# Six borrowed exponential tiles, shared first casts and marks, a later first v, and a new order of engines and transfers in a fused routing-attention and gated feed-forward kernel

## The chip, the core and the metric

The kernel runs on one core of a Trainium2 chip. A core has a matrix engine (TensorE, "PE" in the profile; "PEld" is its weight load), a vector engine (VectorE, "DVE"), a scalar engine (ScalarE, "ACT"), a general engine (GpSimd, "POOL") and an engine that issues most transfers (SyncE, "SP"). Each engine works through its own list of instructions in order; semaphores tie the lists together. The metric is the device time of one execution in microseconds (us). Where several executions are compared, the median counts.

## The reference

Attention with 4 batches, 8 heads, 768 tokens and 64 columns per head. A query sees only those keys whose nearest centroid (of 16 per head) is its own. The result, 3072 rows of 512 columns, goes through a feed-forward layer with a softmax gate and a layer norm.

```python
q_assign = np.argmax(np.einsum('bhsd,hcd->bhsc', q_n, c_n), axis=-1)
k_assign = np.argmax(np.einsum('bhsd,hcd->bhsc', k_n, c_n), axis=-1)
mask = q_assign[:, :, :, None] == k_assign[:, :, None, :]
scores = np.where(mask, scale * np.matmul(q, k.transpose(0, 1, 3, 2)), -1000000000.0)
attn = softmax(scores);  x = matmul(attn, v) as rows of 512
h = x @ w_in                                  # 512 -> 1024
solu = h * softmax(h)
ln = (solu - mu) / np.sqrt(var + 1e-06) * g_ln
return ln @ w_out                             # 1024 -> 512
```

## The kernel before

**Routing inside the matmul.** The kernel builds no mask. Under the 64 columns of q and k it puts 16 rows that hold a 1 at the token's own cluster, so that one matmul with 80 (or 96) contraction rows gives the score plus a large bias where the clusters agree. These rows are called marks here.

**The steps and their names.** Two heads form a pair, so there are 16 pairs, numbered batch.pair. The text `ORDER` names each step by two or three letters, and gives for each engine the order in which its steps are issued; `Weave.queues` (L111) turns a text into a list, and `Weave.run` (L125) emits the steps by a planned start. The table `AWAY` (L74) moves single steps to another engine than their usual one. What stands in `ORDER` is therefore the order on the chip.

| step | what it does | lines |
|---|---|---|
| `ld`, `lv`, `lo`, `li`, `lg` | loads of q and k, v, w_out, w_in, g_ln | L367-403, L526, L548-566 |
| `tp`, `xa` | batch 0: transposes of q or k on PE into the region `hreg`, and the copy to `xt` | L383, L390 |
| `xt` | later batches: transpose on DVE | L405 |
| `ca` | cast of `xt` into the score operand `qk` | L424 |
| `cp`, `cb`, `cq`, `cf` | transposes of the centroids and the two copies made of them | L863-878 |
| `cl`, `tb`, `mx`, `oh`, `ot`, `pl`, `bl` | assignment: scores against centroids, transpose, maximum, one-hot, transpose back, the marks put in place (`place`, L499), a blank | L439-524 |
| `S`, `E`, `V`, `N` | score bank, exponential, attention times v, normalisation | L595-650 |
| `tx`, `h`, `hm`, `ex`, `u`, `tu`, `bn`, `ag`, `at`, `al`, `y`, `sc`, `ou` | the feed-forward part of one block of 128 rows | L678-802 |
| `su`, `sk`, `me`, `ce`, `wi` | w_out centred, w_in cast | L552-590 |
| `fl`, `wm` | idle matmuls | L818, L858 |

**How it is tiled.** There are 294 score banks `S` with as many exponentials `E`, 192 products `V`, and 24 feed-forward blocks. The first 24 banks (pair 0.0) have 384 columns, the other 270 have 512. A score bank is a PSUM tile of a ring of three, so `S` number i waits for `E` number i-3 (L1037). An exponential goes to a tile of a ring of nine in SBUF (`ep`, L212), so `E` number i waits for the `V` that read number i-9 (L1042). `cl`, `cp`, `cq` and `y` share a single PSUM bank (`ps_m`), which a `y` holds until its `sc`.

**The start.** Pair 0.0 is treated in two halves of 384 tokens, so that its first score banks can begin early. The prologue (L805-857) issues the eight small loads of q and k on SP and ACT and then `load_v(0, 0)` (L811). For each half, two transposes and two copies lead to `cl`, then to `tb`, `mx`, `oh` and `ot` on DVE, and then to four marks `pl` (two of k, two of q). In the kernel before, every bank of the first half needs all four (L1033):

```python
            nd |= {f"pl{ts[1 - x]}.{x}.{part}" for x in range(2)
                   for part in ((hh,) if apart(b, p) else range(2))}
```

**Order.** For all engines the order is written out by hand in `ORDER` (L28-73). Each queue is in order: a step that waits holds all steps behind it on its engine.

Of the kernel before, what the change touches and what calls it, by code (L numbers as in the profile page):

```python
# [11 lines left out]
BF16 = mybir.dt.bfloat16  # L12
# [10 lines left out]
class Weave:  # L23
# [6 lines left out]
        ld4 lv si ld4 lv lg ld4 lv2 ld4 lo2 ld4 lo ld3 lo ld3 li4 tx ld3 lv3 tx ld4 tu ld9 lv ld tu  # L30
        tx ld3 tu ld3 ou ld2 ou ld tu ld12 tu ld4 lv ld2 ou tx ld3 tu ou ld2 tx lv ld tu ld4 tx ld
        tu ou2 ld lv ld4 tu ld4 tu ld ou ld7 pl ou ld lv2 ld3 tu lv tx ou tu lv pl ld4 ou2 tx lv tu
        tx ou tu pl2 tu2 tx tu tx ou2 tx ou tu tx2 ou tu2 ou2 tu2 ou6
    """
    ORDER["POOL"] = """
        po z ca2 pl2 cv z bl pl2 ca z ca pl2 ca z2 ca3 cv ca cv ca pl3 sg ca cv2 pl3 ca2 gs pl ca cv
        ca wi ca pl2 wi3 bl ca pl2 cv at cv pl ca pl al bl at cv ca pl ca pl cv ca3 al at ca al ca
        at ca pl2 bl cv pl2 ca4 at ca2 al ca pl2 bl pl2 cv2 ca3 al at pl2 bl pl2 ca pl al ca3 at cv
        at pl ca pl2 ca2 pl al cv2 bl cv2 pl2 ca pl al pl at al at pl2 ca3 at al bl cv pl2 bl cv2
        ca3 pl5 al cv3 at al ca2 cv ca cv ca2 at ca2 pl ca al pl2 at2 pl3 at ca cv al at2 al2 at2 al  # L40
        at al3 at al2 at2 al2
    """
    ORDER["PE"] = """
        wm tp2 cp tp cl tp fl5 cl fl4 S3 tp2 S2 tp S cq S tp S2 tp2 S2 V3 S cl S tp2 V3 S gt S tp S
        tp S2 cl S2 V2 S V S2 tp S2 tp S2 V2 S V S2 cl S2 V2 S V2 S3 V S2 V2 S2 V S cl S3 su S2 V3 S
        V S3 V3 S2 V S su S2 V S V3 S3 me S3 V4 S3 cl S3 V4 S2 h S h S2 h S h S2 V3 S2 V h S h V S V
        S h S V S V S h S2 V3 S2 V h S2 h V2 S y3 S2 h3 S3 y V3 h V S2 V2 S cl S3 h2 S2 V3 S y2 S V
        h2 S V y2 S h S V h S2 h S y3 S2 y V3 h S3 cl V2 S V S y S2 y2 S3 V3 S y S2 V3 S2 cl S V S2
        V2 S h S2 V2 S V S h S2 V2 cl V2 S3 y2 S V S2 V y S2 y V2 S3 h2 S V h S h S2 V h S V S V y2
        S h V y2 S2 V S h3 S cl V S2 V2 S h V cl S3 h2 V y V S3 y2 V S h V3 S y S h S2 h2 S3 V2 y h  # L50
        S V S2 y V3 y S3 h3 y S3 V3 S h S V S V cl S V S h S cl V2 S3 y V2 S y S2 y V2 S3 h y V S3 V
        h V2 S3 cl S2 V2 S y3 S2 y S V3 S V S y S2 V S V3 S2 y2 S3 y V2 S2 h V2 S3 h3 S V S2 V y S V
        h2 V2 S y S2 y V y S h2 S3 cl h V S2 V3 S h V2 S3 h2 S y S2 V h S2 V y2 V4 S3 y h S2 h V h V
# [12 lines left out]
        u ag N cv hm sc bn u N hm ag bn N bn u bn2 hm ag2 N bn u bn2 N ag hm bn u N ag hm bn2 u bn2
        hm sc u N ag2 bn tx hm bn sc u bn ag hm bn tu ag u2 bn2 ag sc
    """
    ORDER["ACT"] = """
        wa xa2 ca2 xa ca2 E12 xa2 E6 xa E58 ex E12 ex E8 ex E8 ex E3 sc E5 ca E2 ex E25 ex E9 sc E6  # L70
        ex E5 sc E2 ex E9 ex E8 ex E9 sc E6 ex E18 ex E21 ex E5 sc E3 ex E9 ex E7 sc E2 ex E7 ex E8
        ex E7 ex E6 sc E ex E2 sc E3 ex E2 sc ex sc ex sc ex tu sc tu2 sc2 oz
# [3 lines left out]
        ca0.0.0.0.0 ca0.0.0.1.1 ca1.3.1.1 sc23.0 tu22.1 tu23.1 xa0.0.1.0 xa0.2.1.0 xa0.2.1.1  # L76
        xa0.3.0.0
    """.split(), "ACT"))
    AWAY.update(dict.fromkeys("""
        bl0.0.1 bl2.2 bl3.1 bl3.2 bl3.3 ca0.0.1.0.0 ca0.1.1.0 ca1.0.0.1 ca3.1.1.0 cv0.0.0 cv0.2.0  # L80
        cv1.2.0 cv2.0.0 cv3.3.0 pl0.0.0.1.1 pl0.1.0.0 pl0.2.1.1 pl0.3.0.0 pl0.3.0.1 pl0.3.1.0 sc0
        sc10 sc13 sc17 sc19 sc2 sc23.1 sc3 sc6 sc8 sc9 tu22.0 zo
    """.split(), "DVE"))
    AWAY.update(dict.fromkeys("""
        ca0.0.1.1.1 pl0.0.0.1.0 pl0.0.1.0.0 pl0.0.1.1.0 pl1.0.0.0 pl1.0.0.1 pl1.0.1.0 pl1.0.1.1
        pl1.1.0.0 pl1.1.0.1 pl1.1.1.0 pl1.1.1.1 pl1.2.0.0 pl1.2.0.1 pl1.2.1.0 pl1.2.1.1 pl1.3.0.0
        pl1.3.0.1 pl1.3.1.0 pl1.3.1.1 pl2.0.0.0 pl2.0.0.1 pl2.0.1.0 pl2.0.1.1 pl2.1.0.0 pl2.1.0.1
        pl2.1.1.0 pl2.1.1.1 pl2.2.0.0 pl2.2.0.1 pl2.2.1.0 pl2.2.1.1 pl2.3.0.0 pl2.3.1.0 pl2.3.1.1
        pl3.0.0.0 pl3.0.0.1 pl3.0.1.0 pl3.0.1.1 pl3.1.0.1 pl3.1.1.0 pl3.1.1.1 pl3.2.0.0 pl3.2.0.1
        pl3.2.1.0 pl3.3.0.1 pl3.3.1.0 pl3.3.1.1  # L90
# [79 lines left out]
def kernel(  # L170
# [328 lines left out]
    def place(b, p, hf, i, part, e):  # L499
# [6 lines left out]
        if apart(b, p):  # L506
            ins = VEC[e].tensor_copy(
                side(b, p, i, part, slice(0, S))[D:D + NC_].bitcast(F32)
                .rearrange("p (t u n) -> p u t n", t=n_t // 2, u=2),
                asg[b, p, hf, "oht"][r.start:r.start + NC_].bitcast(F32)  # L510
                .rearrange("p (u t n) -> p u t n", t=n_t // 2, u=2))
        elif e == "SP":
            ins = nc.sync.dma_start(out=dst, in_=src.unsqueeze(1).to_broadcast([NB, 2, n]))
        else:
            ins = VEC[e].tensor_copy(dst.bitcast(F32), src.bitcast(F32).unsqueeze(1)  # L515
                                     .to_broadcast([NB, 2, n // 2]))
# [76 lines left out]
    es, sps_, opss, xs = {}, {}, {}, {}  # L593

# [10 lines left out]
    def expo(n, k):  # L605
        w = wide(n, k)
        es[n, k] = ep.tile([P, 512], BF16, name="e")
# [203 lines left out]
    load_v(0, 0)  # L811
# [47 lines left out]
    for j in range(sum(int(x or 1) for x in re.findall(r"\bfl(\d*)", wv.ORDER.get("PE", "")))):  # L859
# [41 lines left out]
    for idx, (b, p) in enumerate(pairs):  # L901
# [18 lines left out]
        for i in range(2):  # L920
# [340 lines left out]
```

## Time and profile before

| what | value |
|---|---|
| median of 3 runs | 224.53 us (224.07 to 224.60) |
| the profiled execution | 223.91 us, of which 221.9 us are the span of the profile |
| PE, DVE, ACT, POOL busy | 96%, 89%, 86%, 57% of the span |
| granted clock of TensorE | 1.00 in every stretch |
| mean transfer rate | 175 GB/s |

The span goes from the first to the last instruction of the program. An engine's busy time is the union of its instructions; matmuls overlap in the array and their ends are modelled, so a busy PE may still wait. A line of the profile names the source line, the engine, the operation and the tiles (written<-read), then how many there were. The chain of waits follows the work that ended last back to what released it. The lines that matter stand in the prediction.

### The profile page before, as it was taken

What the parts mean: (1) busy time and instruction counts of PE and PEld (TensorE: products, weight loads), DVE (VectorE), ACT (ScalarE), POOL (GpSimd) and SP (SyncE); (2) the same over time, 40 slices, a digit from 0 to 9 for tenths busy, and PEclk for the clock granted to TensorE, in tenths of its full rate; (3) what the DMA queues carried; (4) which work ended last, traced back from release to release, by engine and by line L of the source; (5) the groups of instructions that cost most, each with busy time, mean ns of one, the idle gap of its engine ahead of it and who ended that gap; (6) DMA issues with size and microseconds to landing.
All of it is one profiled execution on the core that took longest, in us unless ns stands there. A gap on an engine that the chain in (4) does not pass through costs nothing.

```text
span 221.9 us, 6576 instructions
## 1 busy us (share of the span) xinstructions
PE 213.1 (96%) x2388; PEld 146.3 (66%) x2420; DVE 197.2 (89%) x359; ACT 191.7 (86%) x372; POOL 127.1 (57%) x247
## 2 busy tenths in 40 slices
PE   7899999999999999999999999999999999999994
PEld 2575656677667678776577666777677777755452
DVE  3899898899999999999998999887999889888982
ACT  3689999999899999998889899999899998983363
POOL 3499842954794999547668534953895403022331
PEclk9999999999999999999999999999999999999999
DMA  6997999999897989899999898499930524396723
GB/s 150 337 324 157 244 226 296 277 237 161 141 214 134 218 140 168 193 193 173 187 240 150 153 184 207 90 171 240 227 74 11 97 57 135 85 136 166 177 80 142
DMA packets 125679, 38.80 MB, mean 175 GB/s; under 512 B 115016, under 2 KB 121168, under 8 KB 125648
## 3 DMA queue, kind: packets, MB, share of 16 engines
q1 hardware_dynamic: 123904, 37.87, 80.4%
q10 hardware_dynamic: 1744, 0.52, 1.0%
q8 instruction: 19, 0.31, 0.6%
q14 instruction: 12, 0.10, 0.1%
HBM read 23.11 MB, written 6.29 MB: 132 GB/s over the span
## 4 chain that ended last, share of the span: by engine, by line
PE 83%; ACT 6%; issue 3%; DVE 2%; DMA 2%; POOL 1%; SPq 1%; ACTq 0%; DVEq 0%; POOLq 0%
PE sps L602 27%; PE hreg L711 17%; PE yps L775 17%; PE ops L625 13%; ACT e L608 5%; PE csc L451 4%; DMA raw<-in_q_dram 2%; PE hreg L387 1%; PE hreg L575 1%; PE hreg L775 1%; PE csc L446 1%; DVE u L730 1%; SPq L370 0%; PE utp L699 0%; ACT xt L394 0%
## 5 line engine op out<-in xcount | busy, mean ns | idle before, releaser
L608 ACT ACTIVATE e<-sps 128x512 bf16<-128x512 f32 (+1 forms) x294 | 150.7, 601 | 11.6 <-PE sps L602 9.6
L602 PE MATMUL sps<-qk 80*128 80x256 bf16 (+5 forms) x636 | 94.2, 264 | 2.0 <-POOL qk L515 0.7
L602 PEld LDWEIGHTS <-qk 80*128 80x128 bf16 (+1 forms) x636 | 60.3, 121 | 28.3 <-issue 9.2
L625 PEld LDWEIGHTS <-e 128*128 128x128 bf16 x1152 | 49.2, 97 | 12.3 <-issue 1.9
L625 PE MATMUL ops<-v,e 128*128 128x65 bf16 x1152 | 53.5, 193 | 0.1
L711 PE MATMUL hreg<-w_in_sb,xT 128*128 128x512 bf16 x173 | 49.1, 379 | 1.1
L775 PE MATMUL yps<-w_out_c,uT 128*128 128x512 bf16 x171 | 46.6, 379 | 0.6
L730 DVE TENSOR_TENSOR u<-e_sb,hreg 128x1024 bf16<-128x1024 bf16 (+1 forms) x25 | 29.1, 1168 | 4.8 <-ACT e_sb L723 4.5
L515 POOL COPY qk<-oht 32x384 f32<-32x384 f32 (+1 forms) x50 | 24.4, 488 | 15.6 <-DVE oht L495 13.4
L741 DVE BATCH_NORM_STATS2 bs<-u 128x6 f32<-128x512 bf16 x48 | 31.5, 677 | 0.1
L717 DVE TENSOR_REDUCE nmax<-hreg 128x1 f32<-128x1024 f32 x24 | 29.0, 1208 | 2.5 <-PE hreg L711 2.2
L723 ACT ACTIVATE e_sb<-hreg,nmax 128x1024 bf16<-128x1024 f32 x24 | 26.9, 1123 | 4.5 <-DVE nmax L717 4.4
L434 POOL CAST qk<-xt 64x768 bf16<-64x768 f32 (+1 forms) x31 | 25.9, 837 | 4.8 <-DVE xt L394 3.3
L775 PEld LDWEIGHTS <-uT 128*128 128x128 bf16 x200 | 18.2, 97 | 11.7 <-issue 0.3
L757 POOL TENSOR_SCALAR esq<-es,mv 128x1 f32<-128x1 f32 x24 | 8.5, 355 | 28.9 <-DVE mv L745 20.7
L436 POOL TENSOR_SCALAR qk<-xt 64x768 bf16<-64x768 f32 (+1 forms) x28 | 22.8, 815 | 1.7
L711 PEld LDWEIGHTS <-xT 128*128 128x128 bf16 x192 | 16.7, 97 | 9.5 <-DVE u L730 0.6
L408 DVE STREAM_TRANSPOSE xt<-raw 128x768 f32<-128x768 f32 x24 | 22.7, 953 | 0.2 <-DMA w_g<-in_moe_w_out_dram 0.2
L751 POOL TENSOR_SCALAR es<-esum 128x1 f32<-128x1 f32 x24 | 5.3, 222 | 27.5 <-ACT e_sb L723 27.0
L650 DVE TENSOR_TENSOR x<-ops,den 128x256 bf16<-128x256 f32 (+1 forms) x39 | 19.0, 486 | 1.3
L760 POOL TENSOR_TENSOR alpha<-esq,halves 128x1 f32<-128x1 f32 x24 | 13.5, 561 | 2.0
L533 POOL CAST v<-vf 128x384 bf16<-128x384 f32 x27 | 13.5, 516 | 0.9 <-DMA vf<-in_v_dram 0.2
(80 smaller groups left out, 165.6 us busy)
## 6 DMA issues: line engine op xcount, KB each, us to landing
vf<-in_v_dram SPq DMA_DIRECT2D x16, 384.0 KB, 4.7
out_dram<-y SPq DMA_DIRECT2D x23, 256.0 KB, 2.6
raw<-in_q_dram SPq DMA_DIRECT2D x50, 96.0 KB, 3.3
raw<-in_k_dram SPq DMA_DIRECT2D x50, 96.0 KB, 2.9
w_g<-in_moe_w_out_dram SPq DMA_DIRECT2D x4, 512.0 KB, 4.6
w_st<-in_moe_w_in_dram SPq DMA_DIRECT2D x4, 512.0 KB, 5.9
raw<-in_q_dram SPq DMA_DIRECT2D x3, 384.0 KB, 6.2
raw<-in_k_dram SPq DMA_DIRECT2D x3, 384.0 KB, 6.7
```

The lines of the kernel that those rows point to most:

```text
L434: VEC[e].tensor_copy(dst, src)
L436: VEC[e].tensor_scalar(dst, src, scalar1=inv_C, scalar2=1.0, op0=Alu.mult, op1=Alu.mult)
L515: ins = VEC[e].tensor_copy(dst.bitcast(F32), src.bitcast(F32).unsqueeze(1) .to_broadcast([NB, 2, n // 2]))
L602: nc.tensor.matmul(sps_[n, k][:, c0:c0 + w], side(b, h // 2, 1, h % 2, keys)[r], side(b, h // 2, 0, h % 2, slice(s0 * P, s0 * P + w))[r])
L608: nc.scalar.activation(es[n, k][:, :w], sps_[n, k][:, :w], Act.Exp, scale=exp_scale, bias=-exp_scale)
L625: nc.tensor.matmul(opss[g][:, s, :VW], es[n, k][:, c0:c0 + P], v1[slot(b, h // 2)][:, h % 2, kt, :VW], start=(kt == 0), stop=(kt == n_t - 1))
L711: uses(nc.tensor.matmul(hreg[:, at(f, f2)[1], :], xTs[f][:, dc, :], w_in_sb[:, dc, f2 * FF2:(f2 + 1) * FF2], start=(dc == 0), stop=(dc == ...
L717: uses(nc.vector.tensor_reduce(ff[f, "nmax"][:], pair_of(f), axis=AXY, op=Alu.max, negate=True), *both(f))
L723: uses(nc.scalar.activation(ff[f, "e"][:], pair_of(f), Act.Exp, bias=ff[f, "nmax"][:], accum_out=ff[f, "esum"][:]), *both(f))
L730: uses(nc.vector.tensor_tensor(ff[f, "u"][:, at_], ff[f, "e"][:, at_], pair_of(f)[:, at_], op=Alu.mult), *banks)
L741: nc.vector.bn_stats(ff[f, "bs"][:, f2, :], ff[f, "u"][:, f2, :])
L775: ins = nc.tensor.matmul(dst, ff[f, "uT"][:, at(f, f2)[0] * (n_fc // 2) + c, :], w_out_c[:, fc, cols], start=(fc == chunks[0]), stop=(fc = ...
```

## The change

1. **Six borrowed tiles.** The first six exponentials are written into `w_in_sb`, which holds the cast w_in only later, in place of the ring of nine. The ring's wait is dropped for the first 15 (`ring_e + n_lent`), and the casts `wi` of w_in get a wait for the products `V` of pair 0.0's first half and for `cp` and `cq`.
2. **First casts and marks.** Marks can also be made on ACT. Three of the first pair's marks are (`pl0.0.0.0.0`, `pl0.0.0.1.1`, `pl0.0.1.1.1`). Four of its eight half casts go to DVE, one stays on ACT. Of the four marks of a half, a first or third key block now waits only for the key mark that covers it.
3. **First v.** Its load leaves the prologue and stands in SP's list behind the loads of q and k of pair 0.1 and of q of pair 0.2.
4. **Order.** All five texts are new. Six more of the scalings `sc` run on ACT, seven more casts `ca` and four more casts of v on DVE, and the four marks that SP made as transfers run on POOL. The numbers of steps on PE are unchanged (732), and its last 97 steps, DVE's last 46 and ACT's last 38 stand in the same order.

```diff
     ORDER["SP"] = """
-        ld4 lv si ld4 lv lg ld4 lv2 ld4 lo2 ld4 lo ld3 lo ld3 li4 tx ld3 lv3 tx ld4 tu ld9 lv ld tu
+        ld4 si ld3 lv ld lg lv2 ld5 lo2 ld3 lo ld2 lv lo ld li3 ld li ld2 tx ld2 lv ld4 tx
...
     ORDER["POOL"] = """
-        po z ca2 pl2 cv z bl pl2 ca z ca pl2 ca z2 ca3 cv ca cv ca pl3 sg ca cv2 pl3 ca2 gs pl ca cv
+        zo sg z po ca pl ca bl pl2 ca2 bl cv pl cv z ca3 pl2 ca pl cv gs ca2 pl2 ca pl z cv
...
     ORDER["PE"] = """
-        wm tp2 cp tp cl tp fl5 cl fl4 S3 tp2 S2 tp S cq S tp S2 tp2 S2 V3 S cl S tp2 V3 S gt S tp S
+        wm tp cp tp fl5 cl tp fl2 tp fl2 cl S tp S2 tp S tp cq tp S2 tp S tp cl S3 tp2 S2 gt
+        V S V S V S V3 S3 cl S3 V2 S V S tp S2 tp S2 V3 S2 tp S tp S V S V S V S V2 S2 cl S3 V2
...
     ORDER["DVE"] = """
-        cn cb xa ca tb mx oh ot pl2 tb mx oh ot xa3 bl cf cv xa zo xa2 tb ca mx oh gk N ot tb pl mx
+        cn xa cb ca3 tb mx oh ot pl ca tb mx oh xa ot cf xa2 cv xa tb mx xa2 oh gk N ot tb
...
     ORDER["ACT"] = """
-        wa xa2 ca2 xa ca2 E12 xa2 E6 xa E58 ex E12 ex E8 ex E8 ex E3 sc E5 ca E2 ex E25 ex E9 sc E6
+        wa xa ca xa2 pl2 E3 xa E xa E pl E70 ex E11 ex E7 sc E3 ex E9 sc E6 ex E8 sc E5 ex
...
+        elif e == "ACT":
+            ins = nc.scalar.copy(dst, src.unsqueeze(1).to_broadcast([NB, 2, n]))
...
+    n_lent = 6
...
-        es[n, k] = ep.tile([P, 512], BF16, name="e")
+        i = BANKS.index((n, k))
+        es[n, k] = (w_in_sb[:, i // 2, 2 * P + i % 2 * HALF:2 * P + (i % 2 + 1) * HALF]
+                    if i < n_lent else ep.tile([P, 512], BF16, name="e"))
...
-    load_v(0, 0)
...
-            add(f"lv{t}", "SP", 0.0, -1990, lambda e: None, [], last_ld[-1:], move=1.3)
+            add(f"lv{t}", "SP", 0.5, first - 34, lambda e: load_v(0, 0), [], ["si"], move=1.3)
...
-            hots = [(i, part) for i in (1, 0) for part in range(2)]
+            hots = ([(1, 0), (0, 0), (0, 1), (1, 1)] if half and not hf else
+                    [(i, part) for i in (1, 0) for part in range(2)])
...
-                   for part in ((hh,) if apart(b, p) else range(2))}
+                   for part in ((hh,) if apart(b, p) else range(2))
+                   if not (halves_of(b, p) and x and kt % 3 == 2 * (1 - part))}
...
-        if i >= ring_e:
+        if i >= ring_e + n_lent:
...
-        add(f"wi{dc}", "POOL", 1.04, 28 + dc, (lambda e, dc=dc: cast_w_in(dc, e)), [f"li{dc}"],
+        add(f"wi{dc}", "POOL", 1.04, 28 + dc, (lambda e, dc=dc: cast_w_in(dc, e)),
+            [f"li{dc}", "cp", "cq"] + [f"V{n}.{j}" for n in GROUPS[0] for j in range(3)],
```

134 lines of the change are left out of this document (74 added, 60 removed).

## The prediction

> **What bounds the kernel now.** I read the page first, for the busy engines and the chain of waits.
>
> ```profile
> span 221.9 us, 6576 instructions
> ...
> PE 213.1 (96%) x2388; PEld 146.3 (66%) x2420; DVE 197.2 (89%) x359; ACT 191.7 (86%) x372; POOL 127.1 (57%) x247
> ...
> PE 83%; ACT 6%; issue 3%; DVE 2%; DMA 2%; POOL 1%; SPq 1%; ACTq 0%; DVEq 0%; POOLq 0%
> ```
>
> PE is the bound as a whole, so a new order can win only where PE does not run. Where that is, the table of stretches says: start:end, then the busy time of PE, PEld, DVE, ACT and POOL, the granted clock and the transfers.
>
> ```profile
> 0.00:10.00 10.00, 7.71 (x46) 3.78 (x47) 5.39 (x22) 4.79 (x9) 3.90 (x18) 1.00 0.83 228
> 10.00:20.00 10.00, 10.00 (x117) 7.23 (x115) 9.49 (x23) 8.87 (x23) 8.99 (x19) 1.00 1.06 296
> 20.00:30.00 10.00, 9.52 (x131) 6.54 (x131) 9.04 (x19) 9.73 (x22) 8.09 (x15) 1.00 0.78 186
> 30.00:40.00 10.00, 9.74 (x133) 5.98 (x126) 9.09 (x20) 9.25 (x19) 4.07 (x6) 1.00 1.07 297
> 40.00:50.00 10.00, 9.83 (x128) 6.92 (x128) 9.37 (x18) 9.68 (x20) 7.44 (x11) 1.00 1.17 241
> 60.00:160.00 100.00, 98.90 (x1136) 70.40 (x1153) 93.28 (x159) 92.87 (x178) 66.52 (x120) 1.00 0.95 181
> ```
>
> From 60 to 160 us PE is busy for 98.90 of 100. Two windows of the chain of waits, 9.6 to 25 us and then 90 to 120 us, show what a busy PE hides:
>
> ```profile
> by line: PE sps L602 28.2%; ACT e L608 26.6%; PE hreg L387 17.2%; PE csc L446 10.2%; PE ops L625 7.1%; ACT xt L394 5.7%; issue 5.3%; POOL qk L515 2.3%; PE cps L865 0.7%
> by line: PE sps L602 32.2%; PE hreg L711 23.2%; PE yps L775 18.6%; PE ops L625 17.3%; PE csc L451 7.8%; issue 1.1%
> ```
>
> The later window is PE but for 1.1% of issue time: whatever is won before it stays won, and nothing more is to be had in it. The early window has a third on ACT (26.6 and 5.7%): there the stream of exponentials paces. So the question is how much earlier that stream starts, whether it runs without gaps, and what the new body breaks.
>
> **Term 1, the first score bank.** The timeline of the start (start, length, engine, line):
>
> ```profile
> 3.94 0.88 PE L387 MATMUL hreg<-ident_f,raw 128*128 128x128 f32 x3
> 5.04 0.52 PE L387 MATMUL hreg<-ident_f,raw 128*128 128x128 f32 x3 [0.23 <-DMA raw<-in_k_dram]
> 5.60 0.48 ACT L394 COPY xt<-hreg 128x384 f32<-128x384 f32 x1 [0.27 <-PE hreg L387]
> 5.71 0.29 DVE L876 TENSOR_TENSOR c_bd<-cps,own 128x128 f32<-128x128 f32 x1 [0.94 <-PE cps L865]
> 6.26 0.53 PE L451 MATMUL csc<-xt,c_bd 128*32 128x192 f32 x8
> 6.37 0.56 DVE L394 COPY xt<-hreg 128x384 f32<-128x384 f32 x1 [0.37 <-PE hreg L387]
> 6.84 0.34 DVE L436 TENSOR_SCALAR qk<-xt 64x384 bf16<-64x384 f32 x1
> 7.11 0.37 DVE L460 STREAM_TRANSPOSE cst<-csc 128x192 f32<-128x192 f32 x1
> 8.36 0.38 DVE L495 STREAM_TRANSPOSE oht<-oh 128x192 bf16<-128x192 bf16 x1
> 8.77 0.58 DVE L515 COPY qk<-oht 32x192 f32<-32x192 f32 x2
> 8.88 0.75 POOL L515 COPY qk<-oht 32x192 f32<-32x192 f32 x2 [0.77 <-DVE oht L495]
> 9.68 0.65 PE L602 MATMUL sps<-qk 80*128 80x384 bf16 x3 [0.72 <-POOL qk L515]
> ```
>
> In the kernel before, `cl` ends at 6.79 but DVE is at its copy and cast, and `tb` starts at 7.11. `ot` ends at 8.74, the second mark of POOL at 9.63, and the first bank starts at 9.68. In the changed order DVE begins with the copy of the first q at 4.82 (0.56, to about 5.4), then the centroids (0.29) and three half casts (0.34 each): 5.41 + 0.29 + 1.02 is 6.72, and with some 0.1 of steps between them 6.85. The centroid transpose stands ahead of k's, which moves those from 5.04 to about 5.1, and their copy on ACT ends at 6.15. PE has five idle matmuls ahead of `cl`, which ends at about 6.85 as before. So `tb` starts at about 6.9, 0.2 earlier, and `ot` ends at 8.5. The marks are then made by three engines side by side; before, DVE and POOL each made two in turn. The first bank no longer needs the fourth. No mark on ACT stands in this trace; it is bounded by DVE's (0.58 for two, so 0.29) and by ACT's copy of as many columns on all partitions (0.48), and I take 0.45, near the row of the same engine. That ends at about 9.1, and the first bank starts at about 9.15 (bounds 9.0 to 9.2): 0.5 gained. ACT makes the fourth mark before the first exponential, which so starts at about 9.6 in place of 10.04: **0.44** (0.4 to 0.75).
>
> The DVE and POOL copies above overlap, DVE from 8.77 to 9.35 and POOL from 8.88 to 9.63, and POOL's pair takes 0.75, as the next POOL pair does against other DVE work (11.02, 0.74, quoted below). [...]
>
> **Term 2, the stream to the 24th exponential.** ACT's timeline, and what POOL and DVE put before pair 0.1:
>
> ```profile
> 10.04 3.56 ACT L608 ACTIVATE e<-sps 128x384 bf16<-128x384 f32 x9 [1.11 <-PE sps L602]
> 14.30 1.26 ACT L608 ACTIVATE e<-sps 128x384 bf16<-128x384 f32 x3 [0.71 <-PE ops L625]
> 15.94 0.86 ACT L394 COPY xt<-hreg 128x384 f32<-128x384 f32 x2 [0.38 <-PE hreg L387]
> ...
> 19.14 0.49 ACT L394 COPY xt<-hreg 128x384 f32<-128x384 f32 x1
> 19.60 5.62 ACT L608 ACTIVATE e<-sps 128x384 bf16<-128x384 f32 x12
> ...
> 11.02 0.74 POOL L515 COPY qk<-oht 32x192 f32<-32x192 f32 x2 [0.40 <-DVE oht L495]
> ...
> 21.63 0.39 PE L602 MATMUL sps<-qk 80*128 80x256 bf16 x2 [0.29 <-ACT e L608]
> ```
>
> Nine exponentials fill the ring; then ACT waits 0.71 for the products (`ops`), and 0.38 later for transposes. With six borrowed tiles the first wait has no cause (the ring now binds at the 16th), and the copies stand elsewhere. ACT's other work in the stretch stays equal: three copies before (0.86 + 0.49 = 1.35), two copies and a mark after (0.96 + 0.45 = 1.41). A stream without gaps would be 0.44 + 0.71 + 0.38 - 0.06 = 1.47 ahead at the 24th. Can the others follow? PE: from the first bank to the 25th it has 24 banks (two take 0.33 in the chain: 4.0 in all), nine products (1.65), eleven groups of transposes (0.33 each: 3.6), two `cl` (0.78 each) and 0.2 of small ones, 11.0 of the 11.95 between 9.68 and 21.63; the new order has nine groups of transposes there, so 10.3, and allows the 25th bank at 19.5. The rows of these chain pieces:
>
> ```profile
> 10.33 0.66 PE hreg L387 x6
> 13.48 0.33 PE sps L602 x2
> 13.81 0.55 PE ops L625 x18
> 14.52 0.78 PE csc L446 x8
> ```
>
> DVE and POOL, busy for 9.49 and 8.99 of the ten, are the tight ones: the second half's `ot` now stands behind a copy and comes 0.5 later, and pair 0.1's marks need `ot` behind two more copies and a normalisation. Walking DVE's new list with these durations, pair 0.1's `ot` ends near 18.9 and its first two marks near 20.2, in time for a stream that is 1.4 ahead, with little to spare. So the term is between 0.44 (only the head is kept) and 1.47. I take **0.9**, the middle, since with two engines at nine tenths some slip is likely. The two groups of transposes that are put off (0.66) go where PE idles: 0.48, 0.26 and 0.17 of each ten from 20 to 50.
>
> **The rest of the change.** The later first v takes the fourth large place on SP's queue:
>
> ```profile
> 5.14 0.47 SPq L375 DMA_DIRECT2D raw<-in_q_dram  x1
> ...
> raw<-in_q_dram SPq DMA_DIRECT2D x3, 384.0 KB, 6.2
> ```
>
> Issued near 5.14 with a landing after 6.2, it is there at 11.4; in the walk of DVE's list its cast comes near 13, so 1.6 us cover it, and nothing is priced. The three loads that it lets pass are queued one place earlier, and feed transposes that PE has no place for before 9.2. What is late next, if a load is, is the third `cl`. The wait added to `wi` is for the products of the first normalisation, and thirty transfers stand ahead of the first w_in load in SP's list: hidden. The body:
>
> ```profile
> L790 ACT ACTIVATE y<-yps,alpha 128x512 f32<-128x512 f32 x13 | 9.0, 694 | 5.6 <-PE yps L775 5.4 <-POOL alpha L760 0.2
> L792 DVE TENSOR_SCALAR y<-yps,alpha 128x512 f32<-128x512 f32 x10 | 7.3, 735 | 0.9 <-issue 0.5 <-POOL alpha L760 0.2 <-PE yps L775 0.2
> L436 DVE TENSOR_SCALAR qk<-xt 64x768 bf16<-64x768 f32 x2 | 1.1, 570 | 0.0
> L533 DVE CAST v<-vf 128x384 bf16<-128x384 f32 x5 | 2.2, 441 | 0.0
> ```
>
> Six scalings more on ACT are 6 x 0.694 = 4.2, in the stretch from 60 to 160 where it idles for 7.1. DVE loses 6 x 0.735 = 4.4 and gets four full casts (2.3), three half ones (1.0) and four of v (1.8): about level. Four marks go from SP's queue to POOL, which idles for a third there. PE's work is the same. I price the body at 0, under cover of that ACT idle time; if it is gone, rival two has the price.
>
> **Sum.** 223.91 - 0.9 = 223.0 for an execution like the profiled one. The median of the runs stands 0.62 above that execution, so I predict **223.6**.
>
> **Rivals.** *One: the head start is swallowed.* PE is busy for 10.00 of 10 between 10 and 20, and DVE for 9.49; if pair 0.1's marks slip as far as the stream gains, the first exponential's 0.44 is all that stays, or less: 224.1 to 224.5, no change that can be told. For it: these two engines; against it: the third on ACT in that window of the chain. *Two: ACT becomes the bound of the body.* Between 60 and 160 it would be busy for 92.87 + 4.2 = 97.1 of 100, and every scaling in its list waits for its `y` and `alpha` (the 5.4 us of waits for `yps` in the row above), with all exponentials queued behind it; PE has three banks as cover. It decides from a loss of 1.6 us on (the 0.9, and 0.67 more), under half of the 4.2. With half of it paid the time is 223.6 + 2.1 = 225.7. For it: the small rest of idle time; against it: the quoted chain from 90 to 120 has no ACT in it. *Three: the full stream.* All 1.47 is kept, and the idle time of ACT from 20 to 50 (0.27, 0.75, 0.32) shrinks with earlier marks by up to 0.9: 224.53 - 2.4 = 222.1.
>
> **How the numbers follow.** What counts as a difference here is 0.3%, 0.67 us. The forecast (222.9 to 223.9) has 0.42, rival three 0.11, rival one 0.24, rival two 0.23. Of the forecast a little falls within 0.67, and of rival three all is faster: faster 0.51, same 0.26, slower 0.23. The range goes from rival three's 222.1 to 225.7 of rival two at half its price; the likeliest case's own is 222.9 to 223.9.
>
> **What would show it.** Right: the first bank near 9.15 and the first exponential near 9.6; no ACT wait for `ops` in the first 20 us; the first bank of 256-column matmuls (pair 0.1) near 20.7; the first `e_sb` exponential of the feed-forward part about 1.4 earlier than now (0.9, and one exponential of 0.5 fewer ahead of it); ACT near 97 in the stretch from 60 to 160 with PE still near 99; the last 20 us as long as now. Wrong: a first exponential after 9.9, a POOL or DVE mark that holds the 25th bank beyond 21.5, or, in the chain of waits from 60 to 160, scalings `y` and exponentials in more than a few per cent.

## The result and the profile after

| | median | runs |
|---|---|---|
| before | 224.15 us | 6 (223.89 to 224.60) |
| after | 226.31 us | 6 (225.71 to 226.71) |
| ratio | 1.0089 | 95% interval 1.0069 to 1.0109 |

The change makes the kernel slower by 0.9%, 2.2 us. The prediction was 223.6, in a range of 222.1 to 225.7, and the measured time lies above that range. The profiled execution of the changed kernel took 226.47 us, 224.3 of them the span (before: 223.91 and 221.9).

The page of the changed kernel:

```profile
span 224.3 us, 6592 instructions
...
PE 216.7 (97%) x2420; PEld 147.1 (66%) x2420; DVE 199.9 (89%) x360; ACT 194.4 (87%) x377; POOL 124.3 (55%) x245
...
PE 84%; DVE 5%; DMA 5%; ACT 2%; issue 2%; POOL 0%; DVEq 0%; ACTq 0%
```

In the chain that ended last, ACT's share went from 6% to 2%, and DVE and transfers came to 5% each, from 2%.

**The head started as forecast.** PE's timeline of the changed kernel, and below it ACT's (start, length, engine, line):

```profile
9.11 0.32 PE L614 MATMUL sps<-qk 80*128 80x384 bf16 x1
13.32 0.91 PE L614 MATMUL sps<-qk 80*128 80x384 bf16 x3
20.44 0.38 PE L614 MATMUL sps<-qk 80*128 80x256 bf16 x2
```

```profile
9.62 1.27 ACT L622 ACTIVATE w_in_sb<-sps 128x384 bf16<-128x384 f32 x3
10.78 0.49 ACT L402 COPY xt<-hreg 128x384 f32<-128x384 f32 x1
...
11.52 0.51 ACT L402 COPY xt<-hreg 128x384 f32<-128x384 f32 x1
...
12.45 0.51 ACT L523 COPY qk<-oht 32x384 bf16<-32x384 bf16 x1
...
13.37 3.75 ACT L622 ACTIVATE e<-sps 128x384 bf16<-128x384 f32 x9
17.28 4.27 ACT L622 ACTIVATE e<-sps 128x384 bf16<-128x384 f32 x10 [0.15 <-PE sps L614]
```

The first bank starts at 9.11 (9.68 before), the first exponential at 9.62 (10.04), and ACT's wait for `ops` is gone. But two copies and a mark stand between ACT's first exponentials. PE, which needs an emptied bank for each new one, spreads three banks over 0.75 us from 13.32 to 14.07, the start of the next group.

**Where the time went.** The stretches of the changed kernel (PE, PEld, DVE, ACT, POOL busy, then clock and transfers):

```profile
10.00:20.00 10.00, 9.94 (x117) 6.66 (x116) 9.31 (x20) 9.59 (x25) 7.51 (x14) 1.00 1.07 335
20.00:30.00 10.00, 8.88 (x125) 6.72 (x126) 9.68 (x18) 8.89 (x19) 7.86 (x14) 1.00 0.94 245
...
40.00:50.00 10.00, 9.65 (x124) 6.88 (x123) 8.84 (x16) 9.97 (x20) 4.68 (x6) 1.00 0.69 127
60.00:160.00 100.00, 99.13 (x1140) 70.21 (x1138) 92.88 (x160) 94.92 (x184) 64.76 (x119) 1.00 0.96 174
```

From 20 to 30 us PE has 8.88 (9.52 before) and DVE 9.68 (9.04). From 60 to 160 PE's busy time rises, to 99.13, and yet time is lost there: a wait of PE's weight loads can lie inside matmuls that count as busy (PE's row at 49.78, quoted below, is busy for all of its 1.65, though the weight loads of its second half wait 0.66 for DVE's transpose), and before's profile lacks 32 of the 2420 matmul records. Busy shares do not find this loss. What finds it is PE's time at equal work: moments at which both kernels have the same set of PE's steps behind them, read from the starts of the score banks in the two profiled executions. (The experiments' expectations also speak of PE's lost time, kept as a ledger. That is the start of a score bank less the work that PE's order has put before it, with each step at the duration that it has where PE runs gapless: a score bank 0.16 to 0.22, a product 0.18, a feed-forward bank 0.43, a group of transposes 0.33, a full centroid product 0.78.)

```
score banks done         0     15     30     40     48     63     83    138    148    159    230    293
before (us)           9.68  17.20  24.02  29.46  33.93  42.14  53.55  89.48  95.80 103.65 150.95 198.31
after (us)            9.11  16.91  23.29  29.42  33.99  42.13  54.09  90.43  96.79 105.59 153.13 200.57
after less before    -0.57  -0.29  -0.73  -0.04  +0.06  -0.01  +0.54  +0.95  +0.99  +1.94  +2.18  +2.26
```

So the head's lead is kept up to 24 us: 0.73 at equal work, and 1.49 for ACT, whose 31st exponential starts at 23.89 (25.38 before). By 29 us it is gone, and at 34 and 42 us the two kernels are level too. (Between 37 and 40 us PE is up to 0.5 ahead for a while, but ACT's exponentials are not, and it does not last.) Then come 0.5 by 54 us, 0.4 by 90, 0.9 at once by 106, and 0.3 behind. Three places show what PE waits for. The first, where the lead goes, as pieces of the chain of waits at 17 to 25 us (start, length, what):

```profile
17.34 0.56 DVE x L664
...
20.12 0.17 DVE qk L515
20.29 0.83 issue
21.12 0.56 DVE xt L402
21.71 0.72 DVE qk L444
22.43 0.48 DVE xt L402
22.93 1.06 DVE w_out_c L487
...
24.13 0.57 DVE x L664
```

```profile
24.74 0.34 PE L639 MATMUL ops<-v,e 128*128 128x65 bf16 x6 [1.07 <-DVE x L664]
```

DVE is late, from the first normalisation to the second, and PE's timeline (the last row) has a wait of 1.07 for that one. Two of DVE's steps before 24 us are longer than elsewhere. DVE's timeline and then POOL's:

```profile
12.65 0.86 DVE L543 CAST v<-vf 128x384 bf16<-128x384 f32 x1
20.12 0.97 DVE L515 COPY qk<-w_out_c 16x384 f32<-16x384 f32 x1
26.51 0.37 DVE L515 COPY qk<-w_out_c 16x384 f32<-16x384 f32 x1
```

```profile
12.48 0.82 POOL L442 CAST qk<-xt 64x768 bf16<-64x768 f32 x1
20.05 0.82 POOL L442 CAST qk<-xt 64x768 bf16<-64x768 f32 x1
26.17 1.08 POOL L515 COPY qk<-w_out_c 16x384 f32<-16x384 f32 x2 [1.49 <-DVE w_out_c L500]
```

The second place, on SP's queue and on DVE at 40 to 50 us: the first x transfer waits from 32.46 to 40.65 for its data, and the k loads of pair 1.1 stand behind it.

```profile
30.46 2.00 SPq L408 DMA_DIRECT2D raw<-in_q_dram  x1
40.65 1.33 SPq L694 DMA_TRANSPOSE xT<-x  x1
42.08 1.13 SPq L408 DMA_DIRECT2D raw<-in_k_dram  x2
...
43.84 1.03 SPq L408 DMA_DIRECT2D raw<-in_k_dram  x2
```

```profile
49.55 0.98 DVE L416 STREAM_TRANSPOSE xt<-raw 128x768 f32<-128x768 f32 x1 [0.73 <-DMA raw<-in_k_dram]
```

```profile
49.78 1.65 PE L459 MATMUL csc<-xt,c_bd 128*32 128x384 f32 x8
```

The centroid product of pair 1.1 takes 1.65 in place of 0.85, since its second half waits for that transpose. The third place, at 102 us, is in the chain of waits from 60 to 160 us: its shares by line, then its pieces at 98 us, then PE's timeline.

```profile
by line: PE sps L614 33.3%; PE yps L789 19.3%; PE hreg L725 17.9%; PE ops L639 17.4%; PE csc L459 7.0%; DMA uT<-u 4.5%; ACT e L622 0.6%; issue 0.2%; ACTq L622 0.0%
...
98.26 4.53 DMA uT<-u
102.84 1.04 PE yps L789 x4
```

```profile
102.84 1.04 PE L789 MATMUL yps<-w_out_c,uT 128*128 128x512 bf16 x4 [0.74 <-DMA uT<-u]
```

`ex5` starts at 95.31 (90.68 before), so `u` of block 5 is transferred from 98.26 on, and `y5` stands for it. At 70 us ACT's timeline has a smaller one, a scaling with exponentials queued behind it:

```profile
69.77 0.69 ACT L804 ACTIVATE y<-yps,alpha 128x512 f32<-128x512 f32 x1 [0.45 <-POOL alpha L774]
```

### The profile page after: what moved, and what is told of

It reads as the page before. It is cut to its first block, busy times and chain, and to the rows that moved or that the text cites. A ratio compares the mean times of both kernels' runs of the same rounds, so it can differ in the third digit from the quotient of the medians.

```text
span 224.3 us, 6592 instructions
## 1 busy us (share of the span) xinstructions
PE 216.7 (97%) x2420; PEld 147.1 (66%) x2420; DVE 199.9 (89%) x360; ACT 194.4 (87%) x377; POOL 124.3 (55%) x245
## 4 chain that ended last, share of the span: by engine, by line
PE 84%; DVE 5%; DMA 5%; ACT 2%; issue 2%; POOL 0%; DVEq 0%; ACTq 0%
PE sps L614 26%; PE yps L789 18%; PE hreg L725 17%; PE ops L639 14%; PE csc L459 5%; DMA uT<-u 4%; ACT e L622 1%; DMA c_all<-in_centroids_dram 1%; PE hreg L395 1%; PE hreg L585 1%; PE hreg L789 1%; ACT w_in_sb L622 1%; DVE u L744 1%; DVE x L664 1%; DVE w_out_c L487 0%
## 5 line engine op out<-in xcount | busy, mean ns | idle before, releaser
L622 ACT ACTIVATE e<-sps 128x512 bf16<-128x512 f32 (+1 forms) x288 | 148.3, 601 | 9.8 <-PE sps L614 7.7
L614 PE MATMUL sps<-qk 80*128 80x256 bf16 (+5 forms) x636 | 98.3, 264 | 0.7
L639 PEld LDWEIGHTS <-e 128*128 128x128 bf16 x1134 | 52.4, 97 | 13.4 <-issue 1.9
L639 PE MATMUL ops<-v,e 128*128 128x65 bf16 x1134 | 57.5, 193 | 1.1 <-DVE x L664 1.1
L725 PE MATMUL hreg<-w_in_sb,xT 128*128 128x512 bf16 x192 | 54.6, 379 | 0.2 <-DVE u L744 0.2
L789 PE MATMUL yps<-w_out_c,uT 128*128 128x512 bf16 x184 | 50.0, 379 | 0.8 <-DMA uT<-u 0.7
L525 POOL COPY qk<-oht 32x384 f32<-32x384 f32 (+1 forms) x52 | 25.6, 493 | 18.1 <-DVE oht L503 8.6
L442 POOL CAST qk<-xt 64x768 bf16<-64x768 f32 (+1 forms) x28 | 23.0, 820 | 5.1 <-ACT xt L402 3.6
L664 DVE TENSOR_TENSOR x<-ops,den 128x256 bf16<-128x256 f32 (+1 forms) x39 | 18.9, 486 | 1.3
L804 ACT ACTIVATE y<-yps,alpha 128x512 f32<-128x512 f32 x19 | 13.1, 689 | 5.4 <-PE yps L789 4.9
L543 POOL CAST v<-vf 128x384 bf16<-128x384 f32 x23 | 11.8, 521 | 7.2 <-DMA vf<-in_v_dram 6.8
```

The costliest lines, as they stand in the source:

```text
L442: VEC[e].tensor_copy(dst, src)
L614: nc.tensor.matmul(sps_[n, k][:, c0:c0 + w], side(b, h // 2, 1, h % 2, keys)[r], side(b, h // 2, 0, h % 2, slice(s0 * P, s0 * P + w))[r])
L622: nc.scalar.activation(es[n, k][:, :w], sps_[n, k][:, :w], Act.Exp, scale=exp_scale, bias=-exp_scale)
L639: nc.tensor.matmul(opss[g][:, s, :VW], es[n, k][:, c0:c0 + P], v1[slot(b, h // 2)][:, h % 2, kt, :VW], start=(kt == 0), stop=(kt == n_t - 1))
L725: uses(nc.tensor.matmul(hreg[:, at(f, f2)[1], :], xTs[f][:, dc, :], w_in_sb[:, dc, f2 * FF2:(f2 + 1) * FF2], start=(dc == 0), stop=(dc == ...
L789: ins = nc.tensor.matmul(dst, ff[f, "uT"][:, at(f, f2)[0] * (n_fc // 2) + c, :], w_out_c[:, fc, cols], start=(fc == chunks[0]), stop=(fc = ...
```

## The experiments

Nearly all are edits of the orders; what moved is shown by step names. Line numbers are some 66 higher in them. They were measured in several sets, each beside the kernel before, whose median was 224.20 to 224.66 there; so the ratio to before is the number to compare. Leads of PE are read at equal work, as above, in the profiled execution.

**Loads of pair 1.1 ahead of tx0.**

```diff
 SP
-ld1.1.0 tx0 ld1.1.1.0 ld1.1.1.1 lv1.0 ld1.1.1.2 ld1.1.1
+ld1.1.0 ld1.1.1.0 ld1.1.1.1 ld1.1.1.2 ld1.1.1 tx0 lv1.0
```

> The changed order with one edit on SP: the four k loads of pair 1.1 stand ahead of the first transfer transpose tx0, which holds SP's queue from 32.5 to 40.6 us. Theory A: the DVE transpose of that pair no longer waits for k near 49 us (0.73), the following cl does not stretch to 1.58, and 0.5 us come off, so 225.8. Rival B: 226.0 to 226.5. A third way: the loads take transfer time from w_in's loads and the first h comes later, above 226.5.

Measured 225.64 us (ratio to before 1.0058, 1.0037 to 1.0080). PE is 0.07 ahead of the changed kernel at the first bank and 0.91 ahead from the 79th on (50.83 for 51.74); the transpose starts at 48.60 without a wait. By the ratios that wait cost about 0.7, on the path.

**y of block 5 later.**

```diff
 PE
-S48.1 V45.1 y5.0 y5.1 h7.0.1 y5.2 S48.2 y5.3 V46.0 V46.1 S49.0 V47.0
+S48.1 V45.1 h7.0.1 S48.2 V46.0 V46.1 S49.0 y5.0 y5.1 y5.2 V47.0 y5.3
```

> The changed order with one edit on PE: the four y steps of block 5 stand 1.2 us of other PE work later, behind two products and two score banks. Theory A (single waits on PE make the loss, and each is worth what the ledger of lost PE time shows): the wait for the transposed u of block 5 near 102 us goes, about 0.95 us come off the changed kernel's 226.3, so 225.4. Rival B (the wait is only where a slow body shows itself, another engine is the real bound): the lost time comes back elsewhere, 226.0 to 226.5.

Measured 226.93 (1.0113, 1.0091 to 1.0136), above both ranges: nothing gained. The wait for uT is gone, and PE waits for ACT, as its timeline says:

```profile
102.75 0.38 PE L680 MATMUL sps<-qk 80*128 80x256 bf16 x2 [0.46 <-ACT e L688]
104.32 0.38 PE L680 MATMUL sps<-qk 96*128 96x256 bf16 x2 [0.65 <-ACT e L688]
```

ACT has a scaling (0.69), a cast that the change gave it (0.84), one exponential and then `ex6` (1.31) in a row.

**That, the loads, and the cast back on POOL.**

```diff
 ACT
-sc4 ca2.1.0.0 E47.2 ex6
+sc4 E47.2 ex6
 POOL
-ca2.1.1.0 pl2.1.1.0
+ca2.1.1.0 ca2.1.0.0 pl2.1.1.0
```

> Three edits to the changed kernel: the four k loads of pair 1.1 ahead of the transfer tx0 (which alone gave 225.64), the y banks of block 5 six steps later (which alone gave 226.93, since ACT took the place of the uT transfer), and the cast ca2.1.0.0, 0.84 us at 101.63, taken back from ACT by POOL, which idles from 100.81 to 102.59. Theory A (the loss at 102 us had two limits, the late uT and ACT's pile of a scaling, the cast and an e_sb exponential; with both lifted it goes): some 0.9 less than with the loads alone, 224.5 to 225.0, and PE loses no more than 0.3 us between 100 and 108. Rival B (a third limit stands behind the two, DVE or the e_sb exponential alone): PE again loses 0.8 or more there, and the time stays at 225.4 to 226.0.

Measured 225.78 (1.0057, 1.0037 to 1.0077), as with the loads alone. Rival B: a third limit takes over, DVE's normalisation, late behind a transpose, a maximum and others.

```profile
102.74 0.54 PE L704 MATMUL ops<-v,e 128*128 128x65 bf16 x12 [0.63 <-DVE x L729]
```

**Second normalisation earlier on DVE.**

```diff
 DVE
-pl0.1.1.1 xa0.3.0.0 ca0.2.1.1 xa0.3.0.1 oh0.2 N1 xa0.3.1.0
+pl0.1.1.1 xa0.3.0.0 N1 ca0.2.1.1 xa0.3.0.1 oh0.2 xa0.3.1.0
```

> The changed order with one edit on DVE: the second normalisation stands ahead of the cast ca0.2.1.1, one copy and one one-hot step. Theory A: PE's wait of 1.07 us at 24.7 us for that normalisation goes; if it is worth its size, 225.3. Theory A': the ledger shows that the changed kernel has made up for this wait by 38 us, since ACT paces there, so the wait goes and the time stays within 0.3 of 226.3. Rival C (the marks of pair 0.2, now 0.7 later, hold PE in its place): no gain and a new wait of score banks for POOL near 27 us.

Measured 226.71 (1.0103, 1.0080 to 1.0127): nothing gained. What stood behind the normalisation is now late instead:

```profile
26.74 0.83 PE L520 MATMUL csc<-xt,w_out_c 128*32 128x384 f32 x2 [0.40 <-DVE xt L468]
```

**Two of DVE's copies on ACT.**

```diff
 DVE
-pl0.1.1.1 xa0.3.0.0 ca0.2.1.1 xa0.3.0.1 oh0.2
+pl0.1.1.1 ca0.2.1.1 oh0.2
 ACT
-E3.5 E4.0 E4.1 E4.2
+E3.5 xa0.3.0.0 E4.0 E4.1 xa0.3.0.1 E4.2
```

> The changed kernel with two of DVE's copies of pair 0.3 (xa0.3.0.0 and xa0.3.0.1, 0.56 and 0.54 us at 21.12 and 22.36) on ACT, behind the exponentials E3.5 and E4.1. Theory A (between 17 and 26 us DVE simply has too much to do, so PE waits for it at 24.74; moving only the normalisation forward moved the wait to 26.7): the normalisation ends about 1.0 earlier, PE's wait of 1.07 at 24.74 shrinks to 0.2 or less, no new one at 26.7, and the time falls by 0.5 to 1.0, to 225.3 to 225.8. Rival B (ACT's lead is what pays for it): the two copies delay the 25th and later exponentials by 0.9, PE waits for ACT instead, and the time stays at 226.0 to 226.6.

Measured 225.27 (1.0030, 1.0011 to 1.0050), 1.0 less than the change by the medians and 1.3 by the ratios. PE's wait of 1.07 goes; 0.17 for ACT stands there. This execution's first bank came 0.52 later than the changed kernel's (9.63), and its 41st 0.10 later (29.52), so 0.4 is gained. (A late start alone does not come back: in the last kernel below, in the changed order, it is 0.48 at both banks.) In the profiled execution 0.7 more comes at 102 us, without an edit there: SP issues the same transfer at 98.42, and `y` starts without a wait, at most 3.7 us later where it had been 4.5.

```profile
98.42 2.27 SPq L815 DMA_TRANSPOSE uT<-u  x1
```

```profile
102.07 1.04 PE L855 MATMUL yps<-w_out_c,uT 128*128 128x512 bf16 x4
```

**Both mended.** The diffs of the loads and of the copies together.

> The changed kernel with the two edits that each gained by itself: the k loads of pair 1.1 ahead of tx0 (225.64) and DVE's two copies of pair 0.3 on ACT (225.27), against 226.3 for the changed kernel. Theory A (two separate losses, at 49 and at 25 us, that add up): 224.3 to 224.9. Rival B (the body after 55 us takes back what is won before, as its waits hang on transfers whose time does not move with PE): 225.2 or more. Where uT of block 5 lands early enough, as it did with the copies on ACT (no wait for it at 102 us), the lower end; where it holds y again for 0.9, the upper.

Measured 224.91 (1.0012, 0.9986 to 1.0037): no longer told from before. The profiled execution (224.35) had the earliest first bank of all, 8.83. PE is 0.85 ahead of before there, 0.68 at 42 us and 0.90 at 53 us: with both waits gone, the lead of the head is kept that far. Then the new body takes it: 0.45 are left at 95 us, 0.04 at 104, and at the end PE is 0.26 behind.

**Block 5 earlier on DVE and ACT as well.**

```diff
 DVE
-ot2.0 tb2.1 N17 hm5 mx2.1 ca2.0.1.1 N18 u5
+ot2.0 hm5 tb2.1 N17 mx2.1 u5 ca2.0.1.1 N18
 ACT
-E43.2 E44.0 E44.1 ex5
+ex5 E43.2 E44.0 E44.1
```

> The two edits before, and for block 5 of the feed-forward part the maximum hm5 on DVE ahead of tb2.1, ex5 on ACT three exponentials earlier, and u5 on DVE ahead of the cast and the normalisation that stood before it; its products on PE had been done at 90 us, 4 us before DVE took the maximum. Theory A (the loss at 102 us comes from DVE and ACT taking block 5 late, so that its transfer is issued at 98.3): tu5 is issued 1.1 or more earlier, PE loses less than 0.4 us from 100 to 108, and the time is 0.4 to 0.9 below the two edits alone where these still show the wait, 223.9 to 224.5. Rival B (a third limit, DVE's normalisation there, which comes 1.2 later for it): PE loses 0.8 or more there as before, 224.5 to 225.3.

Measured 226.82 (1.0099, 1.0062 to 1.0137), worse: a miss for both. The maximum now holds the centroid transpose behind it, and PE waits there; the uT wait is not gone either.

```profile
94.97 0.59 PE L855 MATMUL yps<-w_out_c,uT 128*128 128x512 bf16 x2 [0.76 <-DVE cst L534]
```

That explains 1.1 of the 1.9 over the version before it. In the profiled execution the start was later too (last section); how often in this kernel is not known.

**The new head with the old body.** The changed kernel's steps up to `S3.5` (PE), `E3.5`, `pl0.1.1.1` (DVE), `pl0.1.0.1` (POOL) and `ld0.3.1`, then the rest in the order and on the engines of before.

> Every step up to the 24th score bank stands as in the changed kernel (borrowed tiles, casts, marks and first v too), every later step in the order and on the engine of the kernel before. Theory A (the new head gains what the forecast said, the new body loses it and more): 0.5 to 1.2 below the kernel before, 223.0 to 223.7. Rival D (the new head's gain is lost in any body, since ACT and DVE pace from 20 to 45 us): within 0.4 of the kernel before, 223.8 to 224.5. Rival E (the new head costs): above 224.6.

Measured 225.19 (1.0044, 1.0024 to 1.0064). PE is 0.14 ahead of before at the first bank (9.54), 0.35 behind at 29 us, 0.55 at 42 us and 0.58 at the last bank, so what is lost is lost before 42 us. Theory A and rival D fall. In the profiled execution the rest of the difference is the last transfer, in the table of transfers (issue to landing), the kernel's first and then that of before:

```profile
out_dram<-e_sb ACTq DMA_DIRECT2D x1, 128.0 KB, 3.0
```

```profile
out_dram<-e_sb ACTq DMA_DIRECT2D x1, 128.0 KB, 1.8
```

**The same with PE's start as before.**

```diff
 PE
-wm tp0.0.0.0 cp tp0.0.1.0 fl0 fl1 fl2 fl3 fl4 cl0.0.0
+wm tp0.0.0.0 tp0.0.1.0 cp cl0.0.0 fl0 fl1 fl2 fl3 fl4
```

> The kernel with the new head and the old body (225.19, against 224.36 before) with PE's first 14 us put back in two places: the five idle matmuls again behind the first centroid product, and the transpose of the centroids again behind that of k. In five profiled executions with the new head PE's matmuls fell from 0.42 to 0.27 us at points from before 4.6 to 6.4 us, and the first score bank came at 9.04 to 9.54 with it; while PE is slow, the five stand ahead of the centroid product at 0.42 each. Theory A (this is the cost of the new head): 224.4 to 224.8. Rival B (the head loses its lead later, where ACT's two copies and mark stand among the first ten exponentials): the time stays at 225.0 to 225.4 with the first bank at 9.1 or before.

Measured 225.53 (1.0065, 1.0038 to 1.0091): theory A falls, and rival B's range is passed too, with the first bank at 9.32. PE ends 0.32 later than before in the profiled execution, and the last transfer again took 2.9.

**The borrowed tiles alone.** The kernel before with `n_lent = 6`.

> The kernel before (its orders and its sharing among engines) with only the first six exponentials kept in w_in's place. Theory A (the stretch from 10 to 20 us was bound by PE, not by the ring of exponentials, so the ring wait of 0.71 that ACT had there was cover): ACT's wait for ops at 14.30 goes, and the time stays within 0.4 of before, 224.0 to 224.8. Rival B, as the prediction had it: the 0.71 is on the path, and the time falls by 0.4 to 0.7, to 223.6 to 224.0. Rival C: the products that read the exponentials from w_in's place, or the w_in loads that now wait, cost: above 224.9.

Measured 224.58 (1.0024, 1.0002 to 1.0047). ACT's timeline has the 0.71 for `ops` gone, and 0.89 for transposes in place of the 0.38:

```profile
12.30 2.73 ACT L687 ACTIVATE e<-sps 128x384 bf16<-128x384 f32 x6
15.93 0.86 ACT L467 COPY xt<-hreg 128x384 f32<-128x384 f32 x2 [0.89 <-PE hreg L460]
```

The copies start at 15.93, as before (15.94): PE sets that time. In the order of before, the ring's wait was cover for PE's work. What it would have cost in the new order, where these copies stand elsewhere, is not shown.

**The old start with the new body.** Before's orders up to PE's 86th score bank (`S24.1`, 55 us, where PE has done the same steps in both kernels; the other engines cut at `E23.2`, `N10`, `at1`, `tu0`), with the borrowed tiles, then the change's.

> The mirror of it: the order and sharing of before up to PE's 86th score bank (with the exponentials kept in w_in's place), and the changed kernel's from there on. Theory A (the changed body behind 55 us loses by itself): 1.5 to 1.9 above before, 225.7 to 226.2, with PE's losses at 72 and 102 us as in the changed kernel. Rival B (these losses come from the state in which the first part leaves the engines, DVE above all): 224.3 to 225.0.

Measured 226.15 beside 224.66 for before (1.0062, 1.0039 to 1.0086). PE is 0.56 behind before at 54 us and 2.15 behind at the last bank, so the new body costs 1.6 of PE's time behind the old start, as it does behind the new one (0.54 to 2.26 is 1.7), with the same wait at 102:

```profile
102.93 1.04 PE L856 MATMUL yps<-w_out_c,uT 128*128 128x512 bf16 x4 [0.69 <-DMA uT<-u]
```

**The mended start with the old body.** The mirror of it, with both edits.

> The changed kernel's order and sharing with the two edits up to PE's 86th score bank (55 us), where PE has done the same set of steps in both kernels, and from there the kernel before's order and sharing. By the lost PE time of the profiled executions the first part is worth 0.9 to 1.0 less than before's (4.0 lost from the first banks to there, less 0.9 of the loads, against 4.4, and a start 0.5 earlier), and the rest as long as before's. Theory A (what the change loses, it loses in two places before 55 us and in the body behind it, and nothing carries over): 223.0 to 223.7, below both kernels. Rival B (the body after the joint needs the state that before's other engines had, the marks and casts further ahead): 224.2 to 225. If the last transfer, ACT's output of e_sb, takes 2.9 to 3.0 us as in the two kernels with the new head and the old body, in place of 1.8, 1.1 is to be added to either.

Measured 227.52 (1.0131, 1.0088 to 1.0174): a miss, and it tells nothing of the first part, for the joint has a wait of its own.

```profile
60.06 0.98 DVE L483 STREAM_TRANSPOSE xt<-raw 128x768 f32<-128x768 f32 x1 [1.94 <-DMA raw<-in_k_dram]
```

**With the joint mended.**

```diff
 SP
-ld1.2.0.2 tu0 lv1.2 ld1.2.0 ld1.2.1.0 ld1.2.1.1 ld1.2.1.2 ld1.2.1
+ld1.2.0.2 ld1.2.0 ld1.2.1.0 ld1.2.1.1 ld1.2.1.2 tu0 lv1.2 ld1.2.1
```

> The kernel of the joint (the changed kernel with the two edits up to the 86th score bank, the kernel before from there), which took 227.5 since SP held the k loads of pair 1.2 behind tu0 at the joint (issued 53.8 to 58.1, landed 59.98) and DVE stood 1.9 us for them; here these four loads stand ahead of tu0, where SP idled from 46.7 to 50.8. Theory A (the joint's loss of 2.9 us was that wait alone, and the first part is really 0.9 shorter than before's): PE loses 0.4 or less between 55 and 62 us, and the time is 223.2 to 224.0, below both kernels by more than can be mistaken. Rival B (what the first part wins is not kept by before's body, or its start is slower on the whole): 224.2 to 225.2.

Measured 225.03 (1.0036, 1.0005 to 1.0068). The wait of 1.94 is gone, but not the joint's whole cost. The profiled execution started late: PE is 0.19 ahead of before at the first bank (9.49), 0.23 ahead at 54 us, and 0.23 behind at 61 us, behind a feed-forward product that waits for `u` on DVE (58.54 to 59.66). The last transfer takes 2.9 in this one too.

**Seven idle matmuls at the start**, on that kernel and on the change itself.

```diff
-lambda e: [idle(FF2) for _ in range(6)]
+lambda e: [idle(FF2) for _ in range(7)]
```

> The same with seven idle matmuls of 512 columns at PE's start in place of six, which closes PE's gap ahead of the transpose of the centroids (0.26 us at 4.9 in the changed kernel). In the profiled executions so far PE's matmuls of 128 columns fell from 0.42 to 0.27 us at points from before 3.8 to 9.1 us, in those with before's order of PE by 5.0 at the latest, in those with the changed order after 4.9 in seven of nine. Theory A (the gaps in PE's work at its start put the rise off): the rise comes by 5.0, and the time is 0.2 to 0.8 below the kernel beside it with a smaller spread among its runs. Rival B (the point of the rise has nothing to do with the gap): the same time within 0.3, or 0.1 to 0.2 more for the later first transpose.

> The changed kernel with seven idle matmuls in place of six and nothing else, to see how much of the change's loss is its start. Theory A (part of the 2.1 us is a later rise of PE's speed): 225.4 to 226.0. Rival B (the loss lies in the three waits at 25, 49 and 102 us and the body): 226.0 to 226.6.

Measured 224.93 (1.0010, 0.9980 to 1.0041) and 226.38 (1.0083, 1.0059 to 1.0107), as without the seventh: the gap at the start is not the cause. The first of the two shows what becomes of the mended start where it comes early (first bank at 8.95). PE is 0.73 ahead of before there and 0.75 ahead at 54 us, and at the joint that goes, nearly all in one wait, after which PE is 0.26 behind:

```profile
59.74 1.47 PE L792 MATMUL hreg<-w_in_sb,xT 128*128 128x512 bf16 x6 [0.66 <-DVE u L811]
```

So where an execution starts early, the mended start wins 0.75 to 0.90, near the 0.9 of the forecast; where it starts late, it won 0.23. Neither body here keeps it. No version here beats the kernel before.

## Why the prediction was wrong

- **Term 1 was right.** First bank 9.11 for 9.15, first exponential 9.62 for 9.6. In the other executions with the new head the first bank came at 8.83 to 9.63, and once at 10.89.
- **Term 2 was won, and lost again at 25 us.** The 256-column banks start at 20.44, 1.2 earlier than before (21.63; 20.7 forecast). Part of that is work put off: "The two groups of transposes that are put off (0.66) go where PE idles" failed, for they stand at 22.41 and 22.96 with PE busy around them. At equal work the lead is 0.73 at 23.3 us, for the 0.9 forecast. The step that failed behind it is the walk of DVE's list, "in time for a stream that is 1.4 ahead, with little to spare". "Pair 0.1's `ot` ends near 18.9 and its first two marks near 20.2" came close (18.79, and POOL's two marks by 19.99), but the walk stopped there. What is late next, DVE's own mark (21.09) and its second normalisation (24.1), was not followed; PE waited 1.07 for the latter, and behind it was level with before (at 29, 34 and 42 us). Moving it forward only moved the wait; two copies less on DVE ended it. Up to 42 us this is what rival one said would be left, with a normalisation in place of the marks.
- **The ring's 0.71 has no shown worth of its own.** With the borrowed tiles alone the wait goes, and the time does not fall.
- **Three of DVE's steps took longer beside casts of POOL, which the walk of DVE's list did not price.** The copy at 20.12 took 0.97, where the one of the same line at 26.51 took 0.37, and ended 0.22 behind POOL's cast (20.05 to 20.87). DVE's cast at 12.65 took 0.86 (the nine of its form 0.461 on the mean) and ended 0.21 behind POOL's (12.48 to 13.30). The one-hot at 22.93, beside POOL's cast from 22.76 to 23.58, took 1.06, while the one of the same line at 28.67 took 0.56. Beside POOL's copies two steps show no lengthening: the copy at 26.51 lies inside POOL's pair (26.17 to 27.25) and took 0.37, and the first marks of DVE (8.55, 0.25) and POOL (8.66, 0.35) ran side by side. The copy at 20.12 and the one-hot are together 1.1 longer than their like, as much as PE's wait at 24.74 (1.07). No run took an overlap away by itself, so it is open whether the overlap is the cause, and how much of DVE's lateness is this and how much the length of its list.
- **"I price the body at 0" is the step that cost most.** It was priced by shares of busy time, with ACT's idle time as cover. ACT was busy for 94.92 of 100, not 97.1, and scalings are not in that chain, so rival two falls as a mechanism, though its 225.7 was the nearest number. It shows once, in small: with the scaling at 69.77 PE's score banks from 69.4 to 72.3 us come 0.4 later than the work between them accounts for (before: 0.02). The rest was in single waits of an order that I did not walk: the k loads behind the first x transfer, on SP's queue (0.5 by 54 us), and then `ex5`, 4.6 later. Behind 54 us the new body costs 1.6 to 1.7, after either start. At 102 us uT, ACT and DVE are all late, so lifting one left a wait of 0.5 to 0.7 for the next.
- **"Whatever is won before it stays won"** holds for before's body: with the new head PE is 0.55 behind at 42 us and 0.58 at the end. For a new order it says nothing, as its waits lie elsewhere.
- The tail is as long as before, and no wait for the first v was seen.

So a gain of 0.9 was forecast for the head and nothing for the rest; up to 42 us nothing is won, and behind it 2.26 are lost. Of the whole difference the loads (0.7) and DVE at 25 us (0.4, with up to 0.7 at 102 us that came along) are shown by taking them away: with both mended the median falls by 1.4 and the ratio to before from 1.0089 to 1.0012. The new body behind 54 us is shown as a whole by the kernel with the old start; its single waits, other than that at 102 us, are not taken apart. Why the same transfer at 98 us took 4.5 us in one kernel's execution and under 3.7 in another's is open.

## What to carry to other kernels

Where an order is new, price it by walking each queue past its waiting steps, transfers too: name for each what is late next, since busy shares hide a wait of 1 us in 100. Read an earlier start at equal work of the bounding engine, not at the first instruction of another. Where removing a wait brings nothing, look for a second and a third limit within a few tenths, and mend the place rather than the wait.

## What the hardware showed beyond that

- **PE's start.** The matmuls of 128 columns at the start fall from 0.42 to 0.27 us at a point that differs between executions. The table of stretches shows clock 1.00 there too, but only because the trace holds no clock record ahead of that point: its first one, at full clock, begins at 4.93 us of the span before the change, at 5.44 after it, and between 3.81 and 9.23 in all seventeen profiled executions. With the new order of PE's start the first bank follows it: 8.83 to 9.04 where the record begins between 4.1 and 4.9, and 9.26 to 9.63 where it begins between 6.0 and 6.8. In the version with three edits a group of three transposes still took 0.90 at 8.23, for 0.55 in the changed kernel, and the first bank came at 10.9 (8.83 in the earliest of these executions):

```profile
8.23 0.90 PE L461 MATMUL hreg<-ident_f,raw 128*128 128x128 f32 x3
```

  The first idle matmul is at 1.17 (before the change, after it and in the version with three edits), and the first clock record begins between 2.6 and 8.1 us behind that. What decides when, no run here shows.

- **The last transfer.** ACT's output of 128 KB at the end took 1.8 us in thirteen of the profiled executions and 2.9 to 3.0 in four, all of kernels with a new head or start and the old body. A fifth of that kind, which differs from one of the four in SP's order alone, ends in 1.8. What decides it is open; 1.1 us is half of this change's effect.
